# Decode attention over a 4096-row cache: the value loads of groups 1 to 30 issued from ScalarE's queue

## The chip, the core and the metric

The kernel runs on one core of one Trainium2 chip. A core has five engines that run their own instruction streams and wait for each other by semaphores: TensorE (PE, matrix products), VectorE (DVE), ScalarE (ACT), GpSimd (POOL) and SyncE (SP). Transfers between the chip's memory (HBM) and the core's on-chip memory are carried out by 16 DMA engines. An instruction on SP or on ACT issues a transfer; what SP issues stands in the profile under queue q1, what ACT issues under q10, and both kinds are carried by the same 16 DMA engines.

The metric is the device time of one execution in microseconds (us), lower is better. The kernel before takes 1305.13 us, the median of three runs (1305.12 to 1305.22).

## What is computed

One decode step for four tokens of width 512. The token vectors are normalized; the normalized x goes through an attention block with 32 heads and a cache of 4096 keys and values per head, and through an MLP block; the outputs are added.

```python
q = (x @ wq).reshape(B, Sq, H, Dh).transpose(0, 2, 1, 3)      # B=4, Sq=1, H=32, Dh=128
scores = einsum("bhqd,bhkd->bhqk", q, k_cache) * Dh ** -0.5   # k_cache: 4 x 32 x 4096 x 128, f32
o = einsum("bhqk,bhkd->bhqd", softmax(scores), v_cache)       # v_cache: the same shape
attention = o.transpose(0, 2, 1, 3).reshape(B, Sq, H * Dh) @ wo
h = gelu(layernorm(x) @ w3) @ w4                              # the part of the MLP that is left for Sq=1
out = A_x + attention + x + h
```

Keys and values are read once each. They are nearly all of the data: of the 561 MB that the kernel reads, 2 x 268 MB.

## The kernel before, in words

**Groups.** The 128 pairs of token and head are worked on in 32 groups of four (NJ = 32, LAST = 31). A group's keys are 8.39 MB, laid out as 128 partitions with 64 KB each; so are its values. On-chip memory holds three such buffers: `ks[0]` and `ks[1]` for keys, group j in `ks[j % 2]`, and one, `vs`, for values. The values of the last group go into `ks[0]`, where group 30's keys were.

**One group, engine by engine.**
- DVE (loop at L300) spreads the group's query over the partitions (L311, L312), then waits for a token of the semaphore `expd` (L314) and for the keys (L315). In two halves it multiplies the keys by the query in place (L320) and sums the products into scores `sc` (L321). After each half it raises `summed` by one (L324). Three small operations (L326 to L328) give a bound for the scores and raise `nm`.
- ACT (loop at L334) takes `nm`, makes four exponentials into `pw` (L339) and raises `go`; takes `pv`, copies TensorE's product `pv` to `os` (L344) and raises `copied`; takes `poz`, copies the group's four outputs and four sums from `poz` to `oz` (L346) and raises `done`. There is one `pw`, and ACT does these steps strictly in this order.
- PE (function `values`, L366, in a loop at L384) takes `go`, gives back one token of `expd` (L368), waits for the group's values (`landed`), multiplies `pw` by the values (L373, 64 instructions in the trace) and raises `pv`; takes `copied`, makes the small products into `poz` (L378, L380).

Two tokens of `expd` lie ready at the start (L291). So DVE may begin group n only when PE has taken `go` of group n-2, which is when the exponentials of group n-2 are there and PE is through with group n-3.

**Who asks for data.** All large loads are issued from SP, in an order written out by hand (L271 to L284). Each issue has its own wait before it, and SP goes through them one after the other:
- keys of group j+2 wait for `SUMMED[j]`, the second half of group j's sums: then `ks[j % 2]` is free (L277);
- values of group j+1 wait for `DONE[j]`, the copy of group j's outputs on ACT (L278);
- the last group's values wait for `SUMMED[30]` (L279), w4 (into `vs`) for `DONE[30]` (L280), and wo (in five parts into `ks[1]`, L284) for `SUMMED[31]`.

Ahead of the loop stand w3, wq, the keys of groups 0 and 1, the values of group 0 (L272) and the keys of group 2 in two halves (L273). The end of the kernel multiplies by w4 (L396) and by wo as its parts land (L410, L152), copies the sum (L421) and stores it (L423).

The two loops' waits on a semaphore are made by this helper, which takes off what it waited for:

```python
285         def take(engine, sem, n=1):
287             engine.wait_ge(sems[sem], n)
288             engine.sem_inc(sems[sem], -n)
```

Of the kernel before, what the change touches and what calls it, by code (L numbers as in the profile page):

```python
# [39 lines left out]
AF = mybir.ActivationFunctionType  # L40
# [4 lines left out]
P = 128  # L45
# [3 lines left out]
G = 4  # L49
PE, DVE, ACT = mybir.EngineType.PE, mybir.EngineType.DVE, mybir.EngineType.Activation  # L50
# [36 lines left out]
def decode_block(ctx: ExitStack, tc: tile.TileContext, x, k, v, wq, wo, w3, w4, out):  # L87
    nc = tc.nc
    B, H, S, DH = k.shape
# [4 lines left out]
    HP = P // G  # L94
    R = G * S // P
    NG = R // 4
    NJ = B * H // G
# [3 lines left out]
    LAST = NJ - 1  # L101
# [4 lines left out]
    def sb(name, *shape):  # L106
        return consts.tile([P, *shape], F32, name=name)

    def bank(name):
        return psum.tile([P, 4 * DH], F32, name=name)  # L110

    ks = [sb(f"ks{n}", R * DH) for n in range(2)]
    vs = sb("vs", R * DH)
# [4 lines left out]
    pw = sb("pw", NG, 32)  # L118
    os = sb("os", 4, DH)
    rs = sb("rs", G)  # L120
# [7 lines left out]
    sc = [sb(f"sc{n}", R) for n in range(2)]  # L128
    tr = [sb(f"tr{n}", HP) for n in range(2)]
    small = sb("small", 2, 2)  # L130
# [6 lines left out]
    pv = bank("pv")  # L137
    pq = [pv, bank("pq")]
    pt = bank("pt")
    poz = bank("poz")  # L140

    kf = k.rearrange("b h s d -> (b h s d)")
    vf = v.rearrange("b h s d -> (b h s d)")

    def rows(flat, j):
        n = G * S * DH
        return flat[j * n:(j + 1) * n].rearrange("(p n) -> p n", p=P)

    def blocks4(start, stop, w, m, src):

        for t in range(4):
            i = nc.tensor.matmul(total[32 * t:32 * t + m, :], w, src[:, P * t:P * t + P], start=start, stop=stop)  # L152
        return i

    do = Steps(tc)
    sems = {n: tc.alloc_semaphore(n) for n in (
        "x", "w3", "wq", "k0", "k1", "landed", "last", "w4", "go", "pv", "copied", "poz", "out",
        "half0", "half1", "nm", "dve", "summed", "expd", "done")}
# [6 lines left out]
    def load(o, i, sem, by, *after, queue="SP"):  # L165
        return do(queue, lambda e: e.dma_start(o, i), *after, done=(sems[sem], 16, by))

    with tc.tile_critical():
# [63 lines left out]
        for c in range(NC):  # L232
            for t in range(4):
                up = lambda e: e.matmul(y[32 * t:32 * t + 32, :FT], x1nT[:, c, :], w3_sb[:, c, t * FT:(t + 1) * FT],
                                        start=(c == 0), stop=(c == NC - 1))
                d = do("PE", up)
# [3 lines left out]
        d = do("DVE", lambda e: e.tensor_mul(u, hs, hs), a)  # L240
        d = do("DVE", lambda e: e.tensor_scalar(u, u, GELU_B, 1.0, op0=ALU.mult, op1=ALU.add), d)
        d = do("DVE", lambda e: e.tensor_mul(u, u, hs), d)
        a = do("ACT", lambda e: e.activation(th, u, AF.Tanh, scale=GELU_A), d)
        d = do("DVE", lambda e: e.tensor_scalar(th, th, 1.0, 0.5, op0=ALU.add, op1=ALU.mult), a)
        d = do("DVE", lambda e: e.tensor_mul(hs, hs, th), d)
        d = do("DVE", lambda e: e.transpose(gt, hs), d)
# [11 lines left out]
        for n in range(2):  # L258
            a = do("ACT", lambda e: e.mul(pw_row[:, n * 4 * DH:(n + 1) * 4 * DH], pq[n], DH ** -0.5), pq_ok)  # L259
        d = do("DVE", lambda e: e.transpose(wide, pw_row), a)  # L260
# [7 lines left out]
        SUMMED = [(sems["summed"], 2 * j + 2) for j in range(NJ)]  # L268
        DONE = [(sems["done"], j + 1) for j in range(NJ)]
# [2 lines left out]
        load(vs, rows(vf, 0), "landed", None, gT_ok, qT_ok, total_ok)  # L272
        parts = [load(ks[0][:, n:n + HALF], rows(kf, 2)[:, n:n + HALF], f"half{i}", 16, (sems["summed"], i + 1))  # L273
                 for i, n in enumerate((0, HALF))]
        for j in range(LAST - 1):
            if j > 0:
                load(ks[j % 2], rows(kf, j + 2), f"k{j % 2}", None, SUMMED[j])  # L277
            load(vs, rows(vf, j + 1), "landed", None, DONE[j])  # L278
        last_in = load(ks[(LAST - 1) % 2], rows(vf, LAST), "last", 16, SUMMED[LAST - 1])  # L279
        w4_in = load(w4_sb, w4.rearrange("(p m) n -> p m n", m=NF), "w4", 16, DONE[LAST - 1])  # L280
        do.wait("SP", [SUMMED[LAST]])
# [3 lines left out]
        def take(engine, sem, n=1):  # L285

            engine.wait_ge(sems[sem], n)
            engine.sem_inc(sems[sem], -n)  # L288
# [5 lines left out]
        d = do("POOL", lambda e: e.memset(g4, 0.0), DONE[LAST - 1])  # L294
# [5 lines left out]
        with nc.Fori(0, NJ // 2, engines=OrderedEngineSet([DVE]), head_slot={DVE: 128}) as j:  # L300
            e, n = nc.vector, 0
# [8 lines left out]
            for s in range(2):  # L310
# [6 lines left out]
                w = R // 2  # L317
# [7 lines left out]
                rm, nm = small[:, s, 0:1], small[:, s, 1:2]  # L325
# [5 lines left out]

        do.wait("ACT", [pw_ok, rs0])
        ozs = oz.rearrange("p n (j s h) -> p s n j h", s=2, h=G)
        with nc.Fori(0, NJ // 2, engines=OrderedEngineSet([ACT]), head_slot={ACT: 128}) as j:  # L334
            for s in range(2):
                take(nc.scalar, "nm")
                for h in range(G):
                    hp = slice(HP * h, HP * h + HP)
                    i = nc.scalar.activation(  # L339
                        pw[hp, :, 4 * h:4 * h + 4], sc[s][hp, :].rearrange("p (g w) -> p g w", w=4), AF.Exp,  # L340
                        bias=small[hp, s, 1:2], scale=1.0, accum_out=rs[hp, h:h + 1])
                i.then_inc(sems["go"], 1)
                take(nc.scalar, "pv")
                nc.scalar.copy(os, pv.rearrange("p (m d) -> p m d", m=4)).then_inc(sems["copied"], 1)  # L344
                take(nc.scalar, "poz")
                nc.scalar.copy(ozs[:, s, :, bass.ds(j, 1)].rearrange("p n o h -> p n (o h)"),  # L346
                               poz[:, 0:2 * G].rearrange("p (n h) -> p n h", n=2)).then_inc(sems["done"], 1)


        LTS = {}  # L350
# [36 lines left out]
        for b in range(B - 1):  # L387
            d = do("PE", lambda e: e.matmul(xb[:, b, :], lts[:, b].rearrange("p h q -> p (h q)"), sel, start=True, stop=True),
                   LTS[b])
# [4 lines left out]
        for m in range(NF):  # L394
            t, g, n = (m, g4[:, m, :], 32) if m < 4 else (m % 4, gT[:, m, :], B)
            nc.tensor.matmul(y[32 * t:32 * t + n, :], g, w4_sb[:, m, :], start=(m < 4), stop=False)  # L396
        d = do("PE", lambda e: e.matmul(xb[:, B - 1, :], lts[:, B - 1].rearrange("p h q -> p (h q)"), sel, start=True,
                                        stop=True), LTS[B - 1])
# [6 lines left out]
        for (c0, c1), sem in zip(wo_cuts, wo_sems):  # L405
            do.wait("PE", [(sem, 16)])
            for c in range(c0, c1):
                if c < 24:
                    t = (c + 2) % 4
                    i = nc.tensor.matmul(y[32 * t:32 * t + B, :], X[:, c, :], wo_sb[:, c], start=False, stop=(c >= 20))  # L410
                else:
                    i = blocks4(False, c == WC - 1, X[:, c, :], B, wo_sb[:, c])
            d = do("PE", lambda e: i)
# [7 lines left out]
        d = do("DVE", lambda e: e.tensor_copy(r, total), d)  # L421
        for t in range(4):
            stored = do("SP" if t % 2 == 0 else "ACT", lambda e: e.dma_start(  # L423
                out.rearrange("b s d -> (b s) d")[:, P * t:P * t + P], r[32 * t:32 * t + B, :]), d,
                done=(sems["out"], 16, 64))
# [31 lines left out]
```

## Time and profile before

| what | value |
|---|---|
| median of three runs | 1305.13 us |
| the profiled execution, its own time | 1305.01 us |
| its span (first to last instruction) | 1303.1 us |
| DVE busy | 1164.2 us, 89% of the span |
| PE busy | 366.4 us, 28% |
| ACT busy | 93.1 us, 7% |
| queue q1 (issued from SP) | 561.00 MB, 99.6% of 16 engines' span |
| queue q10 (issued from ACT: x, and half of the output) | 0.01 MB |
| keys, issue to landing, median of 31 | 42.2 us |
| values, issue to landing, median of 31 | 26.9 us |

The profile is one execution. Times are in us. "DVEq", "SPq" and "ACTq" are an engine's instruction queue: a line such as "SPq L166" is an issue of a transfer at line 166, and "<-DVEq L288" behind a wait says that the instruction was let go by the queue's own wait at line 288, the helper `take`. Line 166 is the helper `load`, so the loads are told apart by the names of their tiles.

### The profile page before, as it was taken

What the parts mean: (1) busy time and instruction counts of PE and PEld (TensorE: products, weight loads), DVE (VectorE), ACT (ScalarE), POOL (GpSimd) and SP (SyncE); (2) the same over time, 40 slices, a digit from 0 to 9 for tenths busy, and PEclk for the clock granted to TensorE, in tenths of its full rate; (3) what the DMA queues carried; (4) which work ended last, traced back from release to release, by engine and by line L of the source; (5) the groups of instructions that cost most, each with busy time, mean ns of one, the idle gap of its engine ahead of it and who ended that gap; (6) DMA issues with size and microseconds to landing.
All of it is one profiled execution on the core that took longest, in us unless ns stands there. A gap on an engine that the chain in (4) does not pass through costs nothing. (4 is left out here: it accounts for less than half of the span.)

```text
span 1303.1 us, 6697 instructions
## 1 busy us (share of the span) xinstructions
PE 366.4 (28%) x2652; PEld 131.4 (10%) x2652; DVE 1164.2 (89%) x324; ACT 93.1 (7%) x330; POOL 2.4 (0%) x12
## 2 busy tenths in 40 slices
PE   3221233321233331133332123332122332113237
PEld 1000111100011110011110011110001111001112
DVE  3499999999999999999999999999999999999990
ACT  1000000000000000000000000000000000000000
POOL 0000000000000000000000000000000000000000
PEclk8655666655666665666665666665566666566668
DMA  9999999999999999999999999999999999999998
GB/s 403 444 422 445 428 439 430 435 430 437 430 428 441 424 445 424 445 424 441 428 439 430 437 430 435 433 428 439 424 445 424 445 424 443 426 439 430 437 422 350
DMA packets 10559, 561.10 MB, mean 431 GB/s; under 512 B 1188, under 2 KB 1204, under 8 KB 1464
## 3 DMA queue, kind: packets, MB, share of 16 engines
q1 hardware_dynamic: 10528, 561.00, 99.6%
q8 instruction: 4, 0.07, 0.0%
q14 instruction: 3, 0.02, 0.0%
q10 hardware_dynamic: 24, 0.01, 0.0%
HBM read 561.00 MB, written 0.01 MB: 431 GB/s over the span
## 5 line engine op out<-in xcount | busy, mean ns | idle before, releaser
L320 DVE TENSOR_TENSOR ks<-ks,qb 128x8192 f32<-128x8192 f32 x64 | 556.3, 8692 | 60.4 <-DVEq L288 55.4
L321 DVE TENSOR_REDUCE sc<-ks 128x64 f32<-128x8192 f32 x64 | 555.9, 8686 | 2.2
L373 PE MATMUL pv<-vs,pw 128*32 128x512 f32 x1984 | 284.3, 737 | 872.8 <-PEq L288 872.8
L373 PEld LDWEIGHTS pv<-vs,pw 128*32 128x32 f32 x1984 | 78.0, 132 | 1054.6 <-issue 1054.6
L344 ACT COPY os<-pv 128x512 f32<-128x512 f32 x32 | 18.8, 586 | 825.1 <-ACTq L288 825.1
L339 ACT ACTIVATE pw<-sc,small 32x128 f32<-32x128 f32 x128 | 51.0, 398 | 278.0 <-ACTq L288 276.8
L378 PE MATMUL poz<-sel,os 128*128 128x4 f32 x256 | 32.8, 252 | 28.2 <-PEq L288 28.2
L378 PEld LDWEIGHTS poz<-sel,os 128*128 128x128 f32 x256 | 31.0, 191 | 56.3 <-issue 56.3
L339 ACT ACTIVATION_READ_ACCUMULATOR pw<-sc,small 32x1 f32 x128 | 23.5, 184 | 0.0
L260 DVE STREAM_TRANSPOSE vs<-pw 128x1024 f32<-128x1024 f32 x1 | 1.2, 1245 | 17.2 <-ACT pw L259 17.2
L421 DVE COPY sc<-total 128x128 f32<-128x128 f32 x1 | 0.3, 290 | 16.4 <-PE total L152 16.4
L326 DVE TENSOR_REDUCE small<-sc 128x1 f32<-128x128 f32 x32 | 9.2, 286 | 4.7
L354 DVE RECIPROCAL rz<-oz 128x96 f32<-128x96 f32 (+1 forms) x2 | 1.1, 552 | 12.4 <-ACT oz L346 12.3
L380 PE MATMUL poz<-rs,ones 128*128 128x4 f32 x64 | 11.7, 253 | 0.0
L312 DVE STREAM_TRANSPOSE qb<-qg 128x128 f32<-128x128 f32 x32 | 10.0, 311 | 1.1
L311 DVE COPY qg<-qT 128x4 f32 x32 | 5.4, 170 | 5.5 <-issue 4.7
L380 PEld LDWEIGHTS poz<-rs,ones 128*128 128x128 f32 x64 | 9.7, 192 | 0.0
L346 ACT COPY oz<-poz 128x8 f32 x32 | 5.3, 166 | 50.9 <-ACTq L288 50.9
L410 PE MATMUL y<-ks,X 128*4 128x512 f32 x48 | 7.8, 818 | 3.5 <-DMA ks<-in_A_wo_dram 3.5
L255 PE MATMUL pv<-ks,X 128*32 128x512 f32 x32 | 5.0, 709 | 12.3 <-DMA ks<-in_A_wq_dram 12.3
L373 PE MATMUL pv<-ks,pw 128*32 128x512 f32 x64 | 8.3, 674 | 0.0
L327 DVE STREAM_TRANSPOSE tr<-small 128x32 f32<-128x32 f32 x32 | 6.8, 212 | 1.1
(72 smaller groups left out, 67.1 us busy)
## 6 DMA issues: line engine op xcount, KB each, us to landing
ks<-in_A_k_cache_dram SPq DMA_DIRECT2D x2, 4096.0 KB, 26.9
vs<-in_B_w_dram SPq DMA_DIRECT2D x2, 3584.0 KB, 13.6
ks<-in_A_wo_dram SPq DMA_DIRECT2D x1, 4096.0 KB, 21.7
ks<-in_A_wo_dram SPq DMA_DIRECT2D x1, 2048.0 KB, 26.3
ks<-in_A_wo_dram SPq DMA_DIRECT2D x1, 1024.0 KB, 28.3
ks<-in_A_wo_dram SPq DMA_DIRECT2D x1, 768.0 KB, 29.7
ks<-in_A_k_cache_dram SPq DMA_DIRECT2D x31, 42.2
vs<-in_A_v_cache_dram SPq DMA_DIRECT2D x31, 26.9
```

Source lines behind the costliest of these rows:

```text
L311: step(e.tensor_copy(qg, pairs[:, s, bass.ds(j, 1)].rearrange("p o n -> p (o n)")))
L312: step(e.transpose(qb.rearrange("p (n m) -> p n m", m=HP), qg.unsqueeze(2).to_broadcast([P, DH // HP, HP])))
L320: step(e.tensor_tensor(out=kt, in0=kt, in1=qb.unsqueeze(1).to_broadcast([P, w, DH]), op=ALU.mult))
L321: step(e.reduce_sum(sc[s][:, c:c + w], kt, axis=AX.X))
L326: step(e.reduce_max(rm, sc[s], axis=AX.X))
L327: step(e.transpose(tr[s], rm.to_broadcast([P, HP])))
L339: i = nc.scalar.activation(pw[hp, :, 4 * h:4 * h + 4], sc[s][hp, :].rearrange("p (g w) -> p g w", w=4), AF.Exp, bias=small[hp, s, 1:2], sc ...
L344: nc.scalar.copy(os, pv.rearrange("p (m d) -> p m d", m=4)).then_inc(sems["copied"], 1)
L373: i = nc.tensor.matmul(pv[32 * t:32 * t + 32, :], pw[:, g, :], vt[:, 4 * g:4 * g + 4, :], start=(g < 4), stop=(g >= NG - 4))
L378: nc.tensor.matmul(poz[:, 0:G], os[:, m, :], sel.rearrange("p (h m) -> p m h", m=4)[:, m, 0:G], start=(m == 0), stop=(m == 3))
L380: nc.tensor.matmul(poz[:, G:2 * G], ones.to_broadcast([P, P]), rs, start=True, stop=True).then_inc(sems["poz"], 1)
L410: i = nc.tensor.matmul(y[32 * t:32 * t + B, :], X[:, c, :], wo_sb[:, c], start=False, stop=(c >= 20))
```

## The change

The values of groups 1 to 30 are no longer issued by SP but by ACT, in ACT's loop: right behind the copy of `pv` to `os` (old L344), ahead of the wait for `poz`. The loop body becomes a function `outputs`, called for 15 pairs of groups in the loop and for the last pair (groups 30 and 31) behind it, with no load there. SP keeps the values of group 0, all keys, the last group's values, w4 and wo, in the old order with the same waits. No size, buffer or computation is changed.

```diff
-        for j in range(LAST - 1):
-            if j > 0:
-                load(ks[j % 2], rows(kf, j + 2), f"k{j % 2}", None, SUMMED[j])
-            load(vs, rows(vf, j + 1), "landed", None, DONE[j])
+        for j in range(1, LAST - 1):
+            load(ks[j % 2], rows(kf, j + 2), f"k{j % 2}", None, SUMMED[j])
...
-        with nc.Fori(0, NJ // 2, engines=OrderedEngineSet([ACT]), head_slot={ACT: 128}) as j:
+        n = G * S * DH
+        nexts = vf[n:n * LAST].rearrange("(j s p n) -> p s j n", s=2, p=P, n=n // P)
+
+        def outputs(s, place, following):
+            take(nc.scalar, "nm")
+            for h in range(G):
+                hp = slice(HP * h, HP * h + HP)
+                i = nc.scalar.activation(
+                    pw[hp, :, 4 * h:4 * h + 4], sc[s][hp, :].rearrange("p (g w) -> p g w", w=4), AF.Exp,
+                    bias=small[hp, s, 1:2], scale=1.0, accum_out=rs[hp, h:h + 1])
+            i.then_inc(sems["go"], 1)
+            take(nc.scalar, "pv")
+            nc.scalar.copy(os, pv.rearrange("p (m d) -> p m d", m=4)).then_inc(sems["copied"], 1)
+            if following is not None:
+                nc.scalar.dma_start(vs, following).then_inc(sems["landed"], 16)
+            take(nc.scalar, "poz")
+            nc.scalar.copy(place, poz[:, 0:2 * G].rearrange("p (n h) -> p n h", n=2)).then_inc(sems["done"], 1)
+
+        with nc.Fori(0, NJ // 2 - 1, engines=OrderedEngineSet([ACT]), head_slot={ACT: 128}) as j:
             for s in range(2):
...
+                outputs(s, ozs[:, s, :, bass.ds(j, 1)].rearrange("p n o h -> p n (o h)"),
+                        nexts[:, s, bass.ds(j, 1)].rearrange("p o n -> p (o n)"))
+        outputs(0, ozs[:, 0, :, NJ // 2 - 1], None)
+        outputs(1, ozs[:, 1, :, NJ // 2 - 1], None)
```

The lines left out at the second "..." are the old loop body, which held the same instructions without the load.

More of the change, by code (lines that the diff above doesn't have):

```diff
@@ L333, in decode_block @@
         ozs = oz.rearrange("p n (j s h) -> p s n j h", s=2, h=G)
-        with nc.Fori(0, NJ // 2, engines=OrderedEngineSet([ACT]), head_slot={ACT: 128}) as j:
-            for s in range(2):
[L336 to L347, printed above, removed]
+        n = G * S * DH
[15 more added lines that the diff above has]
+        with nc.Fori(0, NJ // 2 - 1, engines=OrderedEngineSet([ACT]), head_slot={ACT: 128}) as j:
+            for s in range(2):
+                outputs(s, ozs[:, s, :, bass.ds(j, 1)].rearrange("p n o h -> p n (o h)"),
+                        nexts[:, s, bass.ds(j, 1)].rearrange("p o n -> p (o n)"))
+        outputs(0, ozs[:, 0, :, NJ // 2 - 1], None)
+        outputs(1, ozs[:, 1, :, NJ // 2 - 1], None)
         LTS = {}
```

## The prediction

> **What bounds the kernel now.** I read the page first: its shares, its DMA queues, its chain.
>
> ```profile
> PE 366.4 (28%) x2652; PEld 131.4 (10%) x2652; DVE 1164.2 (89%) x324; ACT 93.1 (7%) x330; POOL 2.4 (0%) x12
> ...
> q1 hardware_dynamic: 10528, 561.00, 99.6%
> ...
> DVE 3%; DMA 2%; SPq 0%; PE 0%; issue 0%; DVEq 0%
> ```
>
> DVE looks like the bound at 89%, but the 16 DMA engines are busy for 99.6%, all of it in one queue. The chain holds only the last 5% of the span, so the order of a group has to come from the timeline of a middle stretch:
>
> ```profile
> 643.50 0.17 ACT L346 COPY oz<-poz 128x8 f32 x1 [1.59 <-ACTq L288]
> 643.69 0.33 SPq L166 DMA_DIRECT2D vs<-in_A_v_cache_dram  x1
> 648.28 0.33 SPq L166 DMA_DIRECT2D ks<-in_A_k_cache_dram  x1
> ...
> 651.93 8.69 DVE L320 TENSOR_TENSOR ks<-ks,qb 128x8192 f32<-128x8192 f32 x1 [2.01 <-DVEq L288]
> ...
> 671.28 9.72 PE L373 MATMUL pv<-vs,pw 128*32 128x512 f32 x64 [27.98 <-PEq L288]
> ...
> 681.15 0.59 ACT L344 COPY os<-pv 128x512 f32<-128x512 f32 x1 [29.93 <-ACTq L288]
> ...
> 683.33 0.17 ACT L346 COPY oz<-poz 128x8 f32 x1 [1.59 <-ACTq L288]
> 683.52 0.33 SPq L166 DMA_DIRECT2D vs<-in_A_v_cache_dram  x1
> ```
>
> Keys land and let DVE go at 651.93, values land and let PE go at 671.28, the keys asked for at 648.28 let DVE go again some 19 us later. PE's starts lie 38.70 apart (632.58 to 671.28). So one load takes **L = 19.35**, whole loads follow each other without a gap, and all of it stands in one queue in the order of asking. That order hides two things: when values are asked for, the queue still has 7 to 8 us of keys in it, and while PE holds the only value buffer, the engines have keys to carry. The queue's own waits:
>
> ```profile
> SPq L166 <- ACT oz L346: 969.3, 31, 34.9
> SPq L166 <- DVEq L324: 228.9, 32, 25.1
> ```
>
> SP waits for the outputs' copy before it can ask for the next keys: the program order holds the keys to one load per value load.
>
> **The change, part by part.**
>
> *The issues on ACT.* 30 issues at 0.33 (SP's rows) to 0.575 (ACT's one issue, of x) each. Behind each stands only the `poz` wait, and PE needs 1.4 for those products (681.85 to 683.1 in PE's rows) while ACT issues. Price nothing; ACT is idle for 825 + 277 us in these waits. Without that cover it would be at most 0.6 on `done`, which nobody awaits before w4. The split loop has the same instructions: nothing.
>
> *The earlier request.* Values are asked for behind the copy that ends at 681.74 and not at 683.52: 1.75 earlier. If the queue still has keys in it, that buys nothing. Nothing to 1.75 x 30 is the bound; I take nothing, by the row q1 at 99.6%.
>
> *Two queues.* This is the term that counts: values no longer stand behind or ahead of keys, they run beside them. The trace before has no two large loads in two queues. The nearest row is a packet of another queue (an instruction fetch) while the keys of group 0 were the only load being carried (wq let PE go at 31.72, these keys let DVE go at 51.99):
>
> ```profile
> DMA packets 26, 1.65 MB, mean 552 GB/s; under 512 B 0, under 2 KB 0, under 8 KB 0
> ...
> q1 hardware_dynamic: 25, 1.64, 126.9%
> q8 instruction: 1, 0.02, 2.1%
> ```
>
> That is the DMA view of 35 to 38 us: the q8 packet got its turn in the middle of a 19 us load. I take from it that an engine changes queues between packets (64 KB here, 8 per engine and load), and that two loads under way **get half the engines' time each**. The bounds are: the later load waits its turn (no change, 1305), and each change of queue costs as that row has it, 2.1% of 3 us x 16 engines = 1.0 us for 16 KB that q1's rate would carry in 0.6, so 0.4 extra.
>
> The Trainium skill (DMA: Bandwidth & Descriptors, "Queues, rings and completion order") agrees on taking turns packet by packet, but gives 9 to 17 descriptors as a typical packet. By that rule a load's 8 rows per engine could pass as one turn, which is the first rival; the q8 row above speaks against it.
>
> *What half speed does to a group.* From a value load's landing to the first packet of the next: 0.2 to PE's start, 9.2 (mean of 9.72, 9.17, 8.60), 0.15 and 0.59 for ACT's copy, 1.5 to the first packet (x was asked for at 0.91 and read at 2.51): **g = 11.7**, in which no values can move. A value load alone takes 19.35, beside keys all the way 38.7. DVE's own pace, where it did not wait, is 36.55 (88.34 to 307.62, six groups), faster than 38.7. Before, SP's order held it back; now nothing does but `expd`, so the keys run ahead and the values, slowed, fall behind.
>
> - *First phase.* Keys take 19.35 of every 36.55, which leaves 47% of the engines: values at least every 19.35 / 0.47 = 41.1. With gaps it is more; the second phase gives 44.8. I take the middle, 42.9. DVE starts group n at 88.3 + 36.55 (n-1), PE group j at 90.7 + 42.9 j. The lead ends when group j+3 on DVE has to wait for PE's end of group j: 9.2 + 2.5 (outputs copied, 681.00 to 683.50) + 2.35 (four exponentials, token) behind PE's start. 161.4 + 36.55 j = 104.8 + 42.9 j gives j = 9. Cost 9 x 4.2 = **38**.
> - *Second phase.* DVE now starts 4.85 after PE's end, takes 35.05 to its second sum (613.23 to 648.28), and keys move 1.5 later: 41.4 behind PE's end, where the values' first packet is 2.3 behind it. So keys start c = 39.1 after each value load's start. Let keys start d before the next value load. They move d alone and share the rest, so the values take 2 (19.35 - d) + d = 38.7 - d, the cycle is 50.4 - d, and the next d is 50.4 - d - 39.1 = 11.3 - d. Two neighbouring cycles have 11.3 between them, so d is 5.65 on average whatever it starts at, and the mean cycle is **44.75**: 6.05 over 38.7, two long and short ones alternating. Groups 9 to 29, 20 x 6.05 = **121**.
> - *End.* SP's wo waits behind w4, which waits for `DONE[30]`, and the last values are in `ks[0]` early. So group 30's values move alone: 19.35 + 11.7 = 31.05, **-7.6**. From PE's start on group 30: 9.2 + 2.7 + 1.5, then w4 and wo (27.8) and 4.6 behind the last landing (1298.5 to 1303.1) = 45.8, before 51.3 (1251.82 to 1303.1): **-5.5**.
>
> Sum: 38 + 121 - 7.6 - 5.5 = 146 on a span of 1303.1, so 1449. The profiled execution is 1.9 longer than its span and 0.1 off the median: **1451 us**, 11% slower.
>
> **The rivals.**
>
> *A load waits its turn (not slower).* If an engine finishes a whole load's 8 packets before it changes queue, the order stays that of before: values asked for 1.75 earlier, behind the keys under way, ahead of the next. Point of decision: the size of a turn, 64 KB or 512 KB per engine. Time 1305, at best the 0.4% that q1 is short of full, 1300. The same comes of it if both queues were one in truth. For it: 99.6% says that any order without gaps costs the same. Against: the q8 packet inside a load. 0.13.
>
> *Sharing with a price.* With 0.4 on each packet of 2.42 while two queues are at work, shared time is 1.17 times as long: the value load takes 45.2 - 1.33 d, the cycle 56.9 - 1.33 d, the next d is 17.8 - 1.33 d, mean d 7.6, mean cycle 46.8. 29 x 8.1 - 13 = 222: 1527. As that factor is above 1, long and short cycles drift apart until the engines stand idle longer, so up to 1570. For it: the q8 row. Against: an instruction fetch is a single cold packet, and value rows lie ready in their queue. 0.20.
>
> *Values get more than half.* With two thirds they take 29.0, the cycle is at most 40.7: 1340 to 1400. Nothing in the profile shows unequal turns. 0.05.
>
> *Faster.* The earlier request shortens the end and the loop has no gaps: 1298 to 1302. 0.02.
>
> **How the numbers follow.** Equal halves: 0.60, with 1425 to 1485 as its own range (PE's share of g between 8.6 and 9.8 moves the mean cycle by 0.3 and the sum by 9; the first phase at 41.1 takes it down to about 1435, with engines out of step a landing waits for the slowest, 1 us on g and 15 on the sum). The range of 8 in 10 adds most of the priced sharing: 1400 to 1560. A difference of 0.2% is about what a measurement of this kernel can tell from no change; faster by more 0.02, within it 0.12 (the first rival and a bit of the last), slower 0.86.
>
> **What would show it.** Right: q10 carries 30 x 8.39 = 252 MB; the DMA share falls to about 1297 / 1449 = 0.90 and the rate to some 387 GB/s; PE's L373 starts lie about 43 apart at first and then alternate around 44.75; DVE stops waiting for keys in the first third and from about group 12 on waits again, now for `expd`, with PE's outputs just before; value loads take 28 to 38 from issue to landing, and behind some landings the DMA row shows empty tenths. Wrong: a steady 38.7 between PE's starts (turns are whole loads), or a share near 99% with a longer span (the price is in the rate, not in gaps).

## The result and the profile after

The changed kernel takes **1464.49 us** (median of four runs, 1461.14 to 1467.06), the kernel before 1305.12 in the same comparison: ratio 1.122, 95% interval 1.1205 to 1.1233. 1451 was forecast. The profiled execution took 1467.06, its span is 1465.3.

From the page of the changed kernel: engines, DMA queues (packets, MB, share of 16 engines), and the chain that ended last.

```profile
PE 364.6 (25%) x2652; PEld 130.8 (9%) x2652; DVE 1164.2 (79%) x324; ACT 93.0 (6%) x330; POOL 2.4 (0%) x12
...
q1 hardware_dynamic: 6208, 309.34, 49.8%
q10 hardware_dynamic: 4344, 251.67, 39.9%
...
DMA 2%; SPq 0%; PE 0%; issue 0%; DVE 0%; ACT 0%
```

The work of the engines is what it was; the two queues together stand at 89.7% instead of 99.6%. Time by stage, in stretches of the changed kernel (columns: stretch, length, PE busy, granted clock, DMA share, GB/s):

```profile
90.00:480.00 390.00, 95.20 (x670) 0.60 0.99 424
480.00:1387.00 907.00, 206.90 (x1480) 0.59 0.87 372
1387.00:1465.00 78.00, 43.56 (x378) 0.78 0.63 263
```

480 is where PE starts group 9 and 1387 where it starts group 29. Up to 480 the DMA engines are full; from there to 1387 they stand idle for 13%, 118 us of 907, and behind it for some 29 of 78. PE falls behind before 480 too, by 41 us against 38.7 a group, but there the engines carry keys ahead instead of idling. Those keys are missing later: it is one loss, seen at PE earlier than at the DMA engines. One group of that second stretch on the timeline (two neighbouring answers; start, length, what):

```profile
982.43 0.33 SPq L166 DMA_DIRECT2D ks<-in_A_k_cache_dram  x1
988.96 0.59 ACT L344 COPY os<-pv 128x512 f32<-128x512 f32 x1 [42.09 <-ACTq L286]
989.11 0.34 ACTq L346 DMA_DIRECT2D vs<-in_A_v_cache_dram  x1
991.14 0.17 ACT L348 COPY oz<-poz 128x8 f32 x1 [1.59 <-ACTq L286]
993.82 8.69 DVE L318 TENSOR_TENSOR ks<-ks,qb 128x8192 f32<-128x8192 f32 x1 [10.13 <-DVEq L286]
...
1023.69 9.53 PE L382 MATMUL pv<-vs,pw 128*32 128x512 f32 x64 [32.75 <-PEq L286]
1028.88 0.33 SPq L166 DMA_DIRECT2D ks<-in_A_k_cache_dram  x1
1033.37 0.59 ACT L344 COPY os<-pv 128x512 f32<-128x512 f32 x1 [40.05 <-ACTq L286]
```

Values asked for at 989.11 let PE go at 1023.69, 34.6 later; over all groups the median from issue to landing is 35.6, where it was 26.9. DVE waits 10 us, and not for keys: its start at 993.82 lies 2.5 behind the outputs' copy, which is the time of four exponentials. That is the `expd` token, so DVE now depends on PE's end. And DVE's sums, 35.06 later, let SP ask for the next keys at 1028.88. What the DMA engines did in the same group, by the DMA view of three stretches: from 1000 to 1010, with both queues at work (queue, packets, MB, share); from 989.1 to 993.4, when the values had just been asked for; and from 1024 to 1028, while PE held the value buffer (packets count where they start).

```profile
q1 hardware_dynamic: 32, 2.10, 48.4%
q10 hardware_dynamic: 32, 2.10, 48.4%
```

```profile
q1 hardware_dynamic: 23, 1.51, 81.0%
```

```profile
DMA packets 0, 0.00 MB, mean 0 GB/s; under 512 B 0, under 2 KB 0, under 8 KB 0
```

Equal packets of both queues when both have work; a wait before the new load's first packet; and nothing at all while PE multiplies and both key buffers are full. SP's waits changed to match: its 969 us for ACT's outputs are gone, and it waits for DVE's sums.

```profile
SPq L166 <- DVEq L322: 1291.0, 32, 47.2
SPq L166 <- ACT oz L348: 82.9, 1, 82.9
```

### The profile page after: what moved, and what is told of

Same layout as the page of the kernel before. It is cut to its first block, busy times and chain, and to the rows that moved or that the text cites. A ratio compares the mean times of both kernels' runs of the same rounds, so it can differ in the third digit from the quotient of the medians.

```text
span 1465.3 us, 6754 instructions
## 1 busy us (share of the span) xinstructions
PE 364.6 (25%) x2652; PEld 130.8 (9%) x2652; DVE 1164.2 (79%) x324; ACT 93.0 (6%) x330; POOL 2.4 (0%) x12
## 5 line engine op out<-in xcount | busy, mean ns | idle before, releaser
L344 ACT COPY os<-pv 128x512 f32<-128x512 f32 x32 | 18.8, 586 | 1153.8 <-ACTq L286 1153.8
L348 ACT COPY oz<-poz 128x8 f32 (+1 forms) x32 | 5.3, 166 | 50.7 <-ACTq L286 50.7
## 6 DMA issues: line engine op xcount, KB each, us to landing
vs<-in_A_v_cache_dram ACTq DMA_DIRECT2D x30, 35.6
```

## The experiments

The theory under test: two queues take turns packet by packet, so values move at half speed beside keys; keys run ahead, and the engines run dry while PE holds the only value buffer. Its rivals: the issues on ACT or their earlier point cost the time; mixing queues lowers the engines' rate; keys running ahead is the whole of it. Each edit is made to the changed kernel, unless said otherwise. Cycles are distances between PE's starts in the profiled execution; "groups 9 to 29" is the mean of those 20.

### One queue again, values asked for early

```diff
-        for j in range(1, LAST - 1):
-            load(ks[j % 2], rows(kf, j + 2), f"k{j % 2}", None, SUMMED[j])
+        for j in range(LAST - 1):
+            if j > 0:
+                load(ks[j % 2], rows(kf, j + 2), f"k{j % 2}", None, SUMMED[j])
+            load(vs, rows(vf, j + 1), "landed", None, (sems["vfree"], j + 1))
...
-                nc.scalar.dma_start(vs, following).then_inc(sems["landed"], 16)
+                nc.scalar.sem_inc(sems["vfree"], 1)
```

> The values of groups 1 to 30 go back to SP's queue, but are asked for at the changed kernel's point (when ACT has taken pv), about 2 us earlier than before. Turns theory (two queues take turns packet by packet, values then move at half speed while keys are under way): one queue, so no turns; 1304 to 1306, 38.7 between PE's starts. Rival 'the earlier request itself disturbs the order': about 1464. Rival 'the engines lose rate when two queues are mixed': also 1305.

Measured 1305.04, ratio to the kernel before 1.000 (0.999 to 1.0009), every cycle up to group 30 between 38.7 and 38.8. The page: `q1` at 99.6% again, values 29.1 from issue to landing instead of 26.9. They are asked for 2.2 earlier and land when they did: the queue is full, the earlier request buys nothing and costs nothing.

### One queue, but ACT's

The keys of groups 3 to 31 and the last group's values move to ACT's queue as well (the loop around it is left out):

```diff
...
             take(nc.scalar, "nm")
+            if keys is not None:
+                nc.scalar.dma_start(ks[s], keys).then_inc(sems[sem or f"k{s}"], 16)
```

> The keys of groups 3 to 31 and the last group's values are issued from ACT too, in front of a group's exponentials, so that one queue, ACT's, carries keys and values in the order of asking. Turns theory: about 1305, up to 1312 because w4 and wo stay on SP and share with the last values. Rival 'issuing large loads from ACT costs (its issues, its loop)': 1464 or more, since ACT then issues twice as many.

Measured 1305.04, ratio 1.000 (0.999 to 1.0009). Its queues:

```profile
q10 hardware_dynamic: 8664, 503.33, 89.2%
q1 hardware_dynamic: 1888, 57.68, 10.3%
```

ACT issues twice as many large loads as in the changed kernel, and nothing is lost. With the run above this takes ACT, its loop and the point of the issue out of the question: what costs is that keys and values stand in different queues.

### The size of a packet

Key loads cut into two of 32 KB rows; value loads so cut; both; key loads in four of 16 KB rows. The edit for the key halves (quarters have // 4 and 64; groups 0 and 1 and POOL's count for group 2, left out here, change likewise):

```diff
+        def keys(j, *after):
+            w = R * DH // 2
+            for n in range(0, R * DH, w):
+                load(ks[j % 2][:, n:n + w], rows(kf, j)[:, n:n + w], f"k{j % 2}", None, *after)
...
-            load(ks[j % 2], rows(kf, j + 2), f"k{j % 2}", None, SUMMED[j])
+            keys(j + 2, SUMMED[j])
...
-                take(e, f"k{s}", 16)
+                take(e, f"k{s}", 32)
```

> The changed kernel, with every key load cut into two loads of 128 rows x 32 KB; values stay at 64 KB rows on ACT's queue. Turns theory (one packet per turn, whatever its size): values get two thirds of the engines beside keys, a value load takes at most 29 instead of 38.7, the cycle at most 40.5: 1330 to 1365. If the engines share by bytes or time and not by packets: 1464. If mixing costs rate per change of queue: slower than 1464, as there are more changes.

> The changed kernel, with every value load on ACT's queue cut into two loads of 128 rows x 32 KB; keys stay at 64 KB rows. Turns theory: values get one third beside keys and fall further behind: 1480 to 1510. Sharing by bytes or time: 1464.

> The changed kernel with keys and values both cut into loads of 32 KB rows. Turns theory: equal packets again, so half each again: 1455 to 1470, as the changed kernel. If each change of queue has a price (0.4 us on a packet was the upper bound of the prediction), twice as many changes show it: up to 1600.

> The changed kernel with every key load of groups 0, 1 and 3 to 31 cut into four loads of 128 rows x 16 KB. Turns theory: values get four fifths beside keys, a value load takes at most 24.2, and with the 4.3 that a value load waits for its first packet beside busy keys (packet records of the changed kernel and of the run with key halves) the cycle is about 0.2 + 9.2 + 0.3 + 4.3 + 24.2 = 38.2, under the engines' 38.7: 1308 to 1330. If that wait grows with the number of key packets ahead of it instead of with their bytes: 1350 or more.

| | us | ratio to before | cycle, groups 0 to 9 | groups 9 to 29 |
|---|---|---|---|---|
| changed kernel | 1464.49 | 1.122 (1.1205 to 1.1233) | 43.24 | 45.38 |
| key halves | 1380.30 | 1.058 (1.0566 to 1.0602) | 40.74 | 41.98 |
| value halves | 1495.48 | 1.147 (1.1444 to 1.149) | 46.23 | 45.39 |
| both halves | 1462.52 | 1.120 (1.118 to 1.1217) | 42.48 | 45.38 |
| key quarters | 1336.16 | 1.025 (1.0221 to 1.0276) | 38.92 | 39.27 |

Turns are packets, whatever their size: with key halves, from 1006 to 1026 us, values move 6.29 MB and keys 2.62.

```profile
q10 hardware_dynamic: 96, 6.29, 72.5%
q1 hardware_dynamic: 96, 2.62, 30.4%
```

(Each queue has 96 turns. 16 of the 96 packets of q1 are not rows: 80 x 32 KB are its 2.62 MB.) Both halves, with twice as many changes of queue, cost nothing over the changed kernel: no price per change. The value halves are slower in the first phase alone; in the second the mean cycle stays at 45.39. That agrees with the prediction's cycle, which does not say so: as long as the keys are through before the values land, the engines move both loads, less the d of keys that went ahead, so a value load takes 38.7 - d whatever its share.

Two of these missed. Key halves were to take 1330 to 1365. A value load there was to take at most 29 and the cycle 40.5, with 1.5 from the issue to the first packet. The view from 1003.2, where values were asked for, to 1007.0 shows that they were not served yet:

```profile
DMA packets 48, 1.57 MB, mean 414 GB/s; under 512 B 0, under 2 KB 0, under 8 KB 0
...
q1 hardware_dynamic: 48, 1.57, 95.9%
```

In these groups the first value packets come 3.7 to 4.5 behind the issue, 4.4 in the mean of the 16 engines (single packets of the trace, which no view prints). With 4.4 in place of 1.5 the cycle is 29 + 0.2 + 9.2 + 0.3 + 4.4 = 43.1, against 42.2 to 43.3 from group 17 to group 27. That fits, but no run isolates it; up to group 17, 14 of the 17 cycles are 38.8 to 41.1, as expected.

Key quarters were to take 1308 to 1330 and took 1336. The wait for the first value packet is 3.4 to 3.5 there, so it does not grow with the number of key packets. The mean cycle is near the engines' 38.7, but it is the keys that are late: DVE waits for them 30 times, 89.4 us in all, and the last group's sums come at 1301.49, where SP asks for wo, 34 later than in the kernel before (1267.53). Of the 28 us that its span is longer than that of the kernel before, 14 lie in the cycles up to PE's start on group 30 (1265.96 for 1251.82) and 14 behind it.

### Keys held back

The old order on SP put back; one token of `expd` instead of two; one token with key halves:

```diff
-            load(ks[j % 2], rows(kf, j + 2), f"k{j % 2}", None, SUMMED[j])
+            load(ks[j % 2], rows(kf, j + 2), f"k{j % 2}", None, DONE[j - 1], SUMMED[j])
```

```diff
-        nc.gpsimd.sem_inc(sems["expd"], 2)
+        nc.gpsimd.sem_inc(sems["expd"], 1)
```

> The changed kernel with SP's old order put back: the keys of group j+2 wait for the outputs of group j-1 as well as for the sums of group j, as they did when the values' issue stood between. If the loss came from keys running ahead alone, this holds them back: near 1305. Turns theory: keys and values are then asked for within 2.5 us of each other, share their whole way (value load about 37 to 38), and the engines stand idle while PE holds the value buffer: cycles towards 49, 1540 to 1575.

> The changed kernel with one token of expd at the start instead of two: DVE begins group n only when the exponentials of group n-1 are there, some 2.3 to 3 us after its sums, so its pace is 38 to 39 instead of 36.55 and keys no longer outrun the engines' 38.7. Turns theory: most of the loss goes, 1360 to 1390. If the engines lose rate by mixing queues, 1464 or a little more.

> e3 and e7 together: keys in 32 KB rows and one token. Turns theory: values get two thirds and keys keep the engines' pace, so the engines are hardly ever idle: 1306 to 1315, near the kernel before and not below it. If the two cures were for the same thing, no better than the better one of e3 and e7.

The old order: 1544.39, ratio 1.182 (1.1802 to 1.1842), from group 4 on nearly all cycles between 47.5 and 48.3: slower than the changed kernel, and the rival "keys running ahead is the whole of it" falls. Keys and values are now asked for 2.2 apart, share their whole way and land within 2.5 us of each other (values let PE go at 1024.20, keys let DVE go at 1026.62), and then the next loads of both wait for PE:

```profile
1024.20 8.62 PE L382 MATMUL pv<-vs,pw 128*32 128x512 f32 x64 [36.97 <-PEq L286]
1026.62 8.69 DVE L318 TENSOR_TENSOR ks<-ks,qb 128x8192 f32<-128x8192 f32 x1 [10.95 <-DVEq L286]
...
1033.12 0.34 ACTq L346 DMA_DIRECT2D vs<-in_A_v_cache_dram  x1
1035.34 0.33 SPq L166 DMA_DIRECT2D ks<-in_A_k_cache_dram  x1
```

From 1023 to 1033 the two queues move 1.05 MB, all of it in the first microsecond, of the 4.3 that fit.

One token: 1371.46 as the median of four runs, but 1346.29 to 1413.50, too far apart for an interval; all four lie under every run of the changed kernel (1461.14 and more) and over the kernel before. In the one trace, that of the longest run, nine of the first twelve cycles are 38.7 to 38.9 and the DMA share up to 560 us is 1.00; from group 16 on long and short cycles alternate as in the changed kernel, with a DMA share of 0.87 from 700 to 1300 us. In this run, holding DVE to the engines' pace delays the loss and does not prevent it. Whether the runs differ by the group at which they tip is not shown, as only one has a trace.

One token and key halves: 1315.14, ratio 1.008 (1.0061 to 1.0095), 0.14 over the upper edge of what was expected, most cycles 38.8. Neither cure alone does this. No version here beats the kernel before, whose one queue is at 99.6%.

### The cycle's terms

The issue placed behind the outputs' copy; half of the products with the values left out (in the changed kernel and in the one before):

```diff
-            if following is not None:
-                nc.scalar.dma_start(vs, following).then_inc(sems["landed"], 16)
             take(nc.scalar, "poz")
             nc.scalar.copy(place, poz[:, 0:2 * G].rearrange("p (n h) -> p n h", n=2)).then_inc(sems["done"], 1)
+            if following is not None:
+                nc.scalar.dma_start(vs, following).then_inc(sems["landed"], 16)
```

```diff
-            for g in range(NG):
+            for g in range(NG // 2):
...
-                                     start=(g < 4), stop=(g >= NG - 4))
+                                     start=(g < 4), stop=(g >= NG // 2 - 4))
```

> The changed kernel with ACT's load issued behind the copy of the outputs, some 2 us later. Two-queue cycle of the prediction: what the values start later, they move longer beside less of the keys, and the mean cycle (38.7 + g + c) / 2 keeps its sum: 1455 to 1475. If the place of the issue in ACT's loop set the time: 30 x 2 = 60 more, 1525.

> The changed kernel with half of the products with the values left out (16 of 32 instructions a group), so that PE holds the value buffer for 4.6 instead of 9.2 us. Cycle of the prediction: g falls by 4.6, c is counted from PE's end and stays, so the mean cycle falls by 2.3: some 20 x 2.3 = 46 less in the second phase and up to 30 in the first: 1375 to 1425. If the loss lay in the rate of the engines or in ACT's issues, it stays at 1464.

> The kernel before with the same half of the products left out. One queue keeps the engines full while PE holds the value buffer, so PE's time is hidden: 1304 to 1306.

Late issue: 1492.84, ratio 1.143 (1.1385 to 1.147): a miss, 28 over the changed kernel where 10 at most were expected and the rival said 60. The mean cycle of groups 9 to 29 did keep its sum (45.85 against 45.38, 9 us in all). What I left out is the first phase: 44.38 against 43.24 a group, 10 us, nearly all of it in its last two cycles (46.3 and 50.1 for 41.1 and 45.6), so the lead ends sooner; why it does is not shown. The end adds some 4, and the three make the 24 between the profiled executions (1490.96 and 1467.06).

Half products, changed kernel: 1406.31, ratio 1.078 (1.0758 to 1.0794), 58 less; the mean cycle of groups 9 to 29 falls by 2.1 to 43.26. PE held the buffer for 5 to 6.5 instead of 8.4 to 10 us. In the mean of these groups the time from PE's start to the next value issue fell by 3.4 (9.4 to 6.0), not by the 4.6 expected; by the cycle that makes 1.7 of the 2.1, and the other 0.4 is open. Half products, kernel before: 1305.55, ratio 1.000 (0.999 to 1.001). The same PE time is free with one queue and on the path with two.

## Why the prediction was right

| step | forecast | measured |
|---|---|---|
| first phase ends with group | 9 | 9: DVE's group 12 waits until 493.45, 5.2 behind PE's end (488.23) |
| first phase, over 38.7 a group | 4.2 x 9 = 38 | 4.54 x 9 = 41 |
| second phase, over 38.7 a group | 6.05 x 20 = 121 | 6.68 x 20 = 134 |
| group 30's cycle | 31.05, -7.6 | 30.97, -7.7 |
| from PE's start on group 30 to the end | 45.8, -5.5 | 46.9, -4.4 |
| sum on the span | 146 | 162 |

**Turns and halves**: right; the packet size runs show it. A turn was one row of 64, 32 or 16 KB, so whole loads, the first rival, fall. The Trainium skill (DMA: Bandwidth & Descriptors, "Queues, rings and completion order") has the turns too, but with 9 to 17 descriptors as a typical packet; by that rule the first rival could have held, and here the measurement decides. **The price per change of queue**, the second rival: none. In the trace's single packets (no view prints them) a 64 KB packet right behind one of the other queue takes 2.42 us, as in the kernel before. **More than half for the values**: only with larger rows than the keys'. **The issues on ACT and the earlier request at nothing**: right.

**The first phase** came out near its price, in part by luck. Its 42.9 was the middle between two numbers and not derived: six of the nine cycles are 38.8 to 41.5, near the lower number, 41.1, and three are 45.6 to 52.2.

**The mean cycle** is the term that was mis-sized: 45.38 for 44.75, with long and short cycles alternating as forecast (44.3 to 44.7 and 45.2 to 46.7 from group 16 on). The single packets of the trace say where the 0.6 lies (means over groups 10 to 28):

- The first packet of keys, on engines that stood idle before it, takes 3.1 and not 2.42: +0.7.
- PE starts 0.8 behind the mean end of the 16 engines' last value packets, where 0.2 was priced; 0.3 of it is the slowest engine's, for which the landing waits: +0.6.
- From PE's start over its end to the next issue of keys it is 49.3, not 9.2 + 4.85 + 35.05 = 49.1: +0.2.
- The first key packets come 1.2 behind that issue in the mean of the engines, not 1.5: -0.3.

Half of these 1.2 counts in the mean cycle: 44.75 + 0.6 = 45.35, against 45.26 over these groups. They come from one trace; no run changes them one at a time. L itself held: in 15 of the 19 groups a value load takes 29.0 or 31.4 from its first to its last packet on an engine, which is 12 or 13 packets of 2.42, eight of its own and four or five of keys.

**The 1.5 to the first packet** was wrong, and did little harm. The row of x that it was taken from shows when x was read; the first packet of x had come 0.96 behind its issue (kernel before). Beside a busy queue, values in the second phase have their first packet 3.4 to 5.2 us after the issue, and 4.1 to 6.4 on the last of the 16 engines (the 16th packet); keys, asked for when the engines are idle, have it after 0.96 (single packets again). In the prediction's sum the values' wait lengthens g and shortens c by the same, so it drops out; in the key halves, where c does not limit, it fits what was missing. ACT's issue, too, comes earlier than priced: 0.15 behind the start of the copy, not behind its end (988.96 and 989.11).

## What to carry to other kernels

When the DMA engines are the bound, the order of one queue is itself a schedule: in this kernel it gave each load the full rate in turn and kept the next one ready while a buffer was held. Here, moving one stream to a second queue added no rate; it let the streams slow each other, in the ratio of their rows, and the stream with a single buffer paid, because its hold time was no longer covered. Before such a move, write down for each stream how long its buffer is held and what the engines carry meanwhile.

## What the runs showed of the hardware

- Two queues with work share the 16 DMA engines row by row: 64 KB against 64 KB gives 2.10 MB each in the same 10 us, 32 KB against 64 KB gives 2.62 MB against 6.29 in 20 us. The size of a row thus sets a load's share.
- A load asked for while the other queue is busy has its first packet 3.4 to 5.2 us after the issue (values of the changed kernel from 536 us on). Into idle engines it is 0.95 to 0.97 for its keys, and 0.97 to 0.98 for the values of the run with the old order. There the first packets take 3.1, not 2.42 us.
- A change of queue between rows that wait in both queues costs nothing that shows: 1462.52 with twice the changes, 1464.49 without, and 2.42 us for a 64 KB packet behind one of either queue. The 0.4 that the instruction fetch seemed to cost in the kernel before does not carry over.
